# One core of Trainium2, attention into a mixture of experts: the first token list from two groups instead of three, and the order of the first weight loads

## The chip, the cores and the metric

The kernel runs on one core of one Trainium2 chip. The core has five engines with an instruction queue each, which run side by side and wait for one another by semaphores: PE (TensorE, matrix products; its weight loads are shown apart as PEld), DVE (VectorE), ACT (ScalarE), POOL (GpSimd) and SP (SyncE, which here only issues DMA transfers). The metric is the device time of one execution in microseconds, with its input and output in device memory; lower is better. The time before is 1149.84 us, the median of three runs (1148.15 to 1151.22).

## The reference

Attention over 8 batches and 8 heads with queries that are averaged in pairs, and behind it a mixture of experts in which each token goes to the one expert with the largest logit:

```python
q_pool = q.reshape(B, H, S // 2, 2, D).mean(axis=3)      # B = H = 8, S = 1152, D = 64
scores = matmul(q_pool, k^T) / sqrt(D)
attn   = exp(scores - max(scores)); attn /= sum(attn) + 1e-9
x      = matmul(attn, v)  ->  reshaped to (4608, 512)     # 8 batches x 576 queries, 8 heads x 64
logits = x @ w_gate + modality_bias[modality_id]          # 8 experts
e      = argmax(logits); gate = softmax(logits)[e]
out    = gate * (relu(x @ w1[e]) @ w2[e])                 # w1: 8 x 512 x 1024, w2: 8 x 1024 x 512
```

Everything is float32 at the interface.

## The kernel before, in words

**Attention.** The work is cut into 32 pairs: a pair is one head of two neighbouring batches. A pair has 18 steps, and Python loops over the 576 steps and writes the instructions of PE, ACT, DVE and POOL in exactly that order (the order of these four engines is set by hand; SP's order is left to the planner of the framework, which places each transfer by when it expects its operands to be ready). In a pair PE makes 24 score tiles (L879, L880), ACT takes the exponential of each (L881, result Pe), and PE multiplies with the values in three products per tile (L938 to L940), the third with the low bits of the exponentials, Pl. Pl is made on ACT for the first two thirds (L862) and on DVE for the rest (L864); in the last pairs the tables LOWS_LAST and P_LIST choose otherwise. The maxima of a pair (L812 on PE, L813 and L821 on DVE) are found one pair ahead; `row` turns them into one row and sends it to the right operand of the scores by a DMA on SP (L793). POOL splits queries and keys into high and low halves (L639, L646, L674) and scales the values (L761).

**Routing.** Eight pairs make one group of 1152 tokens (two batches, all heads); there are four groups, 0 to 3. `on_two` (L1449 and on) stores finished heads to a scratch tensor xs, and when a group's last head is stored, it appends the generator `route(g)` to the list `side`: it adds the logits up, finds each token's expert and its position within the expert. Behind group 2 it appends `first_list`, behind group 3 `other_list`. `first_list` counts how many full blocks of 256 tokens each expert has so far (`first_blocks`, L371 and on), places the tokens (`place`, L444 and on), and turns the places into lists of token numbers with small matrix products (`listing`, L519 and on; its operands in `operands`, L492 and on; `indices`, L542 and on). The result, the lists giA and siA of the first NA = 6 blocks, is what the first gathers of the expert stage need. `other_list` makes the lists of all other blocks from all four groups, later, beside the first six blocks.

**The side loop.** At the end of each step the attention loop advances the first generator of `side` once (L1143 to L1148). The number that it yields is how many steps pass before the next advance. So `route` (with rs = RS[g]) and the list are spread over the steps, a few small DVE or POOL instructions at a time, and each generator of the queue begins when the one ahead of it has ended. A negative yield, T_LIST, means "not before that step counted from the end of attention".

**The passage to the experts.** One step ahead of the last pair `early` takes over the buffers of raw queries, keys and values. `gather_first` first drains whatever is left in `side`, then POOL gathers the first block's tokens with giA (L1173). The first NF = 4 weight tiles of the first block are loaded by SP into the freed buffers (`load_first`, L1479 to L1483, which reads the block's expert from ownerA); ACT and DVE split them in the last pair (L1487, L1489).

**Experts.** 18 blocks of 256 tokens and one of 128 follow, each with eight weight tiles of 512 KB, gathered tokens, two matrix products in three parts each, and a scatter.

Of the kernel before, what the change touches and what calls it, by code (L numbers as in the profile page):

```python
# [9 lines left out]
F32 = mybir.dt.float32  # L10
# [12 lines left out]
P = 128  # L23
# [16 lines left out]
NR = 4  # L40
W3 = 3 * SQ
BANK = W3 // 4
T_LIST = -127
PL = 2
RS = (4, 4, 2, 2)
SLOW_P = 1
SLOW = 3
LAG = 3
# [2 lines left out]

LOWS = (((0, 1152, 'A', 2), (1152, 1728, 'D', 3)), ((0, 1152, 'A', 2), (1152, 1728, 'D', 3)))
LOWS_LAST = (((0, 864, 'D', 1), (864, 1728, 'D', 3)),)
P_LIST = {26: 0, 27: 0}
LOWS_LIST = [tuple(((0, 1152, 'A', 2), (1152, 1728, e, 3)) for e in x) for x in ('DDA', 'DA', 'A')]
D0 = 5
T_RT = 24
# [35 lines left out]
T = BATCH * SQ  # L93
DM = H * D
E = 8
F = 1024
XW = DM + 2
NT = 9
# [19 lines left out]
T_W0 = (1, 3, 2, 3)  # L118
# [7 lines left out]
NA = 6  # L126
# [35 lines left out]
class Router:  # L162
# [112 lines left out]
    def route(self, g, eng):  # L275

        nc, sm, rs = self.nc, self.sm, RS[g]
        while self.added[g] < H // 2:
# [165 lines left out]
    def place(self, nt, late):  # L444

        nc, sm = self.nc, self.sm
        be = lambda a: a.unsqueeze(1).broadcast_to([P, nt, E])
        yield
        wide = lambda i: sm.tile([P, nt, E], F32, name=f"ohp{nt}_{i}") if late else sm.tile([P, 3, NT, E], F32, name=f"wide{i}").rearrange("p q t e -> p (q t) e")
        oh = wide(0)  # L450
        nc.vector.tensor_tensor(oh, self.exp[:, 0:nt].unsqueeze(2).broadcast_to([P, nt, E]), be(self.ie), op=ALU.is_equal)
        yield
        w = wide(1)
        new = lambda name: sm.tile([P, NTT], F32, name=name)[:, 0:nt]

        def pick(o, of):

            nc.vector.scalar_tensor_tensor(w, oh, float(TB), be(of), op0=ALU.mult, op1=ALU.mult)
            yield
            nc.vector.tensor_reduce(o, w, op=ALU.add, axis=AX.X)  # L460
            yield

        lim, row, ok = new("lim"), new("row"), new("ok")
        yield from pick(lim, self.na)
        yield from pick(row, self.full if late else self.cumA[:, 0:E])
        nc.vector.tensor_tensor(row, row, self.pos[:, 0:nt], op=ALU.add)
        if late:
            yield from pick(ok, self.done)
            nc.vector.tensor_tensor(ok, self.pos[:, 0:nt], ok, op=ALU.is_ge)
            more = new("more")  # L470
            yield from pick(more, self.half)
            nc.vector.tensor_tensor(more, more, ok, op=ALU.mult)
            nc.vector.tensor_tensor(row, row, more, op=ALU.add)
        nc.vector.tensor_tensor(ok, self.pos[:, 0:nt], lim, op=ALU.is_ge if late else ALU.is_lt)
        yield
        nc.vector.scalar_tensor_tensor(row, row, float(2 * T), ok, op0=ALU.add, op1=ALU.mult)
        yield
        ri = sm.tile([P, NTT], I32, name="ri")[:, 0:nt]
        nc.vector.tensor_copy(ri, row)
        yield  # L480
        lo, hi = (sm.tile([P, NTT], I32, name=f"{x}i")[:, 0:nt] for x in ("lo", "hi"))
        nc.vector.tensor_single_scalar(lo, ri, P - 1, op=ALU.bitwise_and)
        nc.vector.tensor_single_scalar(hi, ri, 7, op=ALU.logical_shift_right)
        yield
        self.lo = sm.tile([P, NTT], BF16, name="lof")[:, 0:nt]
        nc.vector.tensor_copy(self.lo, lo)
        self.hi = sm.tile([P, NTT], F32, name="hif")[:, 0:nt]
        nc.vector.tensor_copy(self.hi, hi)
        yield
        nc.vector.tensor_single_scalar(self.hi, self.hi, -float(2 * T // P), op=ALU.add)  # L490
# [65 lines left out]
    def first_list(self):  # L556

        for _ in self.first_blocks():
            yield 1
        for _ in self.place(3 * NT, False):  # L560
            yield PL
        yield T_LIST
        acc = self.con.tile([P, 2, 2 * NA], F32, name="accA")
        yield from self.listing(3, 2 * NA, acc)
        self.idxA = self.indices(2 * NA, acc, "A")

    def other_list(self):
# [7 lines left out]
def attention(tc, ctx, att, ident, npairs, xpool, on_two, on_split, on_scale, jobs, side, set_pm, started, ahead, hip):  # L575
# [3 lines left out]
    nc = tc.nc  # L579
# [4 lines left out]
    sm = ctx.enter_context(tc.tile_pool(name="asm", bufs=3))  # L584
# [190 lines left out]
    def row(p, mp, u0, u1):  # L775

        n = u1 - u0
        m9 = sm.tile([P, 9], F32, name="m9")
        nc.vector.tensor_reduce(m9[:, 0:n], mp[:, u0:u1], op=ALU.max, axis=AX.X, negate=True)

        def finish():
            pt = some(0) if p else small()
            nc.tensor.transpose(pt[0:n, 0:P], m9[:, 0:n], ident)
            if now[0] > NSTEP:
                later_end(FD, lambda: put(pt))
            else:
                put(pt)

        def put(pt):
            mr = sm.tile([9, P], F16, name="mr", bufs=1)  # L790
            made.add((p, f"row{u1}"))
            nc.vector.tensor_scalar(mr[0:n], pt[0:n, 0:P], 1.0 / ROW, 16.0 * math.log(PSC) / ROW, op0=ALU.mult, op1=ALU.add)
            done = (nc.sync if p or u0 else nc.scalar).dma_start(out=B2[p % 2][D:D + 1, 2 * S + u0 * P:2 * S + u1 * P], in_=mr[0:n])  # L793
            if turns:
                with tc.issue_after(done.ins):
                    while turns:
                        turns.pop(0)()
        return finish
# [43 lines left out]
    def scores(p, j, r):  # L842
# [9 lines left out]
        s["P", j, r] = (word(F16, 1), Pl, i % NR)  # L852
        lows = LOWS_LAST if p == npairs - 1 else LOWS_LIST[P_LIST[p]] if p in P_LIST else LOWS if p else LOWS0
        lows = lows[i % len(lows)]
# [114 lines left out]
                on_two(p // 2, x2)  # L969
            later(XD, lambda: split_x(p, x2))  # L970

    turns = []
    now, flushed = [0], [-1]
    free = [0] * NR
    todo, at_end = {}, {}
# [8 lines left out]
    def at(t, p, fn, end=True):  # L984
        if 0 <= p < npairs:
            (at_end if end else todo).setdefault(max(t, 0), []).append(fn)
# [120 lines left out]
    if ahead:  # L1107
        last = (npairs - 1) * NSTEP
        room = []

        def early():
            a, *r = [pa.tile([P, S], F32, name="raw" + x) for x in "qqkkv"]
            room.extend(r)
            ahead[0](a)

        at(last + T_G0, 0, early)
        at(last + T_X0, 0, lambda: running.append(ahead[1](lambda: ps_max.tile([P, 512], F32, name="pm"))))
        for i in range(NF):
            at(last + T_W0[i], 0, lambda i=i: ahead[2](i, room[i]))
            at(last + T_W1[i], 0, lambda i=i: later_end(W1D, ahead[3](i)))  # L1120
    running, wait = [], 0
    for t in range(NSTEP * npairs):
        p, c18 = divmod(t, NSTEP)
        now[0] = t
        if jobs and c18 in JOBS:
            running.append(jobs.pop(0))
        for a in ORD[t % len(ORD)]:
            if a == "J":
                running[:] = [g for g in running if next(g, DONE) is not DONE]
            elif a == "F":  # L1130
                flush(t)
            elif a == "M":
                advance(mxq, 1)
            elif a == "X":
                advance(mxq, 3 if t < T_F else 1 if t < X_ALL or t % (X_IN if t < X_SOME else 4) == 0 or len(mxq) > 1 else 0)
            elif a == "N":
                scq.append(scores(p, *divmod(c18 // 3, 3)))
            elif a == "s":
                advance(scq, 1)
            elif a == "v":  # L1140
                advance(pvq, 2 if len(pvq) > 2 else 1)
        ends(t)
        if side and t >= wait:  # L1143
            r = next(side[0], DONE)
            if r is DONE:
                side.pop(0)
            else:
                wait = t + (r or 1) if (r or 1) > 0 else NSTEP * npairs + r  # L1148
# [14 lines left out]
def parts(j):  # L1163

    return range(2 if j < NBF else 1)


def gather_x(nc, rt, j, tile_):

    x = []  # L1170
    for h in parts(j):
        x.append(tile_(h))
        nc.gpsimd.indirect_dma_start(out=x[h][:, :], out_offset=None, in_=rt.xs[0:3 * NT * P if j < NA else T, :],  # L1173
                                     in_offset=bass.IndirectOffsetOnAxis(ap=index(rt, j, h)[0], axis=0))
    return x

# [260 lines left out]
def attention_moe(tc, att, ids, w_gate, bias, w1, w2, out):  # L1437
    nc = tc.nc
    with ExitStack() as ctx:
# [3 lines left out]
        rt = Router(tc, ctx, ident)  # L1443
# [3 lines left out]
        jobs, side, first = [], [], {}  # L1447

        def on_two(n, x2):  # L1449
            g, cc = divmod(n, H // 2)  # L1450
            eng = nc.gpsimd if n == NPAIR // 2 - 1 else nc.sync
            rt.store(g, cc, x2, eng)
            if cc == H // 2 - 1:
                side.append(rt.route(g, eng))
                if g == 2:
                    side.append(rt.first_list())
                if g == 3:
                    side.append(rt.other_list())
# [32 lines left out]
        ahead = (gather_first, turn_first, load_first, split_first) if NPAIR == BATCH // 2 * H else None  # L1491
# [54 lines left out]
```

## Time and profile before

| what | before |
|---|---|
| median of three runs | 1149.84 us (1148.15 to 1151.22) |
| the profiled execution, its own time | 1147.58 us |
| its span on the chip | 1145.8 us |
| granted TensorE clock, mean | 0.995 |
| attention, first to last exponential | 18.6 to 737.3 us |
| busy share PE, DVE, ACT, POOL | 97%, 85%, 80%, 37% |

A window of the profile is a stretch of the span, in microseconds from its start; for each engine it shows the busy time and, in brackets, how many instructions began in it. The pairs of attention can be told apart in it: each has 24 exponentials on ACT (L881), so pair p begins with exponential 24 p, and within a pair each three steps hold four of them. A "step" of the trace below is meant in that sense. An entry of a group of instructions gives line, engine, operation, output and inputs, shapes, count, busy time and mean duration in ns, and idle time ahead of it with what ended it. The durations on DVE overlap a little at their ends, so that they add to somewhat more than the busy time.

### The profile page before, as it was taken

The numbers are of one execution on the slowest core, as the hardware profiler recorded it, in microseconds if no ns is written. First come the engines' busy times: TensorE is split into PE (matmuls) and PEld (weight loads), VectorE is DVE, ScalarE is ACT, GpSimd is POOL, SyncE is SP. The second block draws the span as 40 slices with busy tenths as digits, with TensorE's granted clock in tenths as the row PEclk, the third lists the DMA queues.
The fourth block names the chain that finished last, engine by engine and source line by source line (L and its number), as shares of the span: only waits on it lengthen the run. The fifth ranks groups of instructions, "written<-read, shape, count | busy, mean of one in ns | idle before, by whom it ended". The sixth has DMA issues, their size and how long they took to land. (4 is left out here: it accounts for less than half of the span.)

```text
span 1145.8 us, 36648 instructions
## 1 busy us (share of the span) xinstructions
PE 1109.3 (97%) x15001; PEld 816.3 (71%) x15001; DVE 978.9 (85%) x1962; ACT 915.3 (80%) x1463; POOL 419.5 (37%) x408
## 2 busy tenths in 40 slices
PE   7999999999999999999999989999999999999995
PEld 3777777777777777777777767866676666766763
DVE  7999999999999999999999999888977667576661
ACT  5999999999999999999999989765656565565561
POOL 7753534444343454434445331232213221211201
PEclk9999999999999999999999999999999999999998
DMA  7776867857858759669668453699989999989970
GB/s 230 204 178 166 190 178 166 196 158 165 194 148 201 190 149 206 152 164 207 165 167 186 129 129 85 226 269 273 287 259 294 291 289 275 280 267 289 263 233 22
DMA packets 175568, 232.65 MB, mean 203 GB/s; under 512 B 92351, under 2 KB 126799, under 8 KB 175392
## 3 DMA queue, kind: packets, MB, share of 16 engines
q1 hardware_dynamic: 169254, 210.45, 70.3%
q0 software_dynamic: 6128, 19.78, 6.4%
q8 instruction: 119, 1.95, 0.7%
q14 instruction: 57, 0.47, 0.2%
q10 hardware_dynamic: 10, 0.00, 0.0%
HBM read 146.11 MB, written 19.18 MB: 144 GB/s over the span
## 5 line engine op out<-in xcount | busy, mean ns | idle before, releaser
L881 ACT ACTIVATE Pe<-psc 128x432 int32<-128x432 f32 x768 | 377.9, 526 | 43.1 <-PE psc L880 34.2
L813 DVE TENSOR_REDUCE mp<-pm 128x1 f32<-128x512 f32 x566 | 372.6, 684 | 14.4 <-PE pm L812 7.2
L938 PE MATMUL xp<-VH,Pe 128*128 128x65 f16 x2880 | 372.6, 193 | 0.0
L940 PE MATMUL xp<-VS,Pl 128*128 128x65 f16 x2880 | 371.9, 193 | 0.4 <-DVE Pl L864 0.4
L939 PE MATMUL xp<-vl,Pe 128*128 128x64 f16 x2880 | 370.7, 192 | 0.0
L939 PEld LDWEIGHTS <-Pe 128*128 128x128 f16 x2880 | 267.6, 98 | 87.6
L879 PE MATMUL psc<-B 128*128 128x432 f16 (+2 forms) x1152 | 304.0, 286 | 1.7 <-ACT Pe L881 1.5
L880 PE MATMUL psc<-B 65*128 65x432 f16 (+2 forms) x1152 | 304.7, 287 | 0.5 <-DMA B<-mr 0.5
L938 PEld LDWEIGHTS <-Pe 128*128 128x128 f16 x2880 | 271.9, 98 | 45.2 <-issue 7.0
L940 PEld LDWEIGHTS <-Pl 128*128 128x128 f16 x2880 | 266.5, 97 | 0.6 <-DVE Pl L864 0.5
L862 ACT ACTIVATE Pl<-Pe 128x1152 f16<-128x1152 uint16 (+1 forms) x190 | 219.3, 1154 | 6.0
L812 PE MATMUL pm<-hi,QB 128*128 128x512 f16 x566 | 213.7, 379 | 8.4 <-DVE mp L813 8.1
L674 POOL TENSOR_TENSOR lo<-rawk,hi 128x576 f16<-128x576 f32 (+1 forms) x68 | 88.0, 1298 | 196.0 <-ACT hi L658 185.6
L761 POOL TENSOR_SCALAR VH<-rawv,sc 128x512 f16<-128x512 f32 (+1 forms) x60 | 103.5, 1735 | 153.0 <-PE xp L940 73.7
L1287 PE MATMUL ph<-xpart,w1l 128*128 128x256 f16 x544 | 148.3, 273 | 0.0
L1285 PE MATMUL ph<-xpart,w1h 128*128 128x256 f16 x544 | 148.3, 273 | 0.0
L1286 PE MATMUL ph<-xpart,w1h 128*128 128x256 f16 x544 | 148.3, 273 | 0.0
L880 PEld LDWEIGHTS <-B 65*128 65x128 f16 x1152 | 112.9, 98 | 25.2 <-issue 2.5
L879 PEld LDWEIGHTS <-B 128*128 128x128 f16 x1152 | 112.5, 98 | 9.2 <-issue 3.8
L1291 DVE SCALAR_TENSOR_TENSOR hl<-ph,hh 128x512 f16<-128x512 f32 x72 | 49.7, 690 | 77.0 <-ACT hh L1290 76.3
L1290 ACT ACTIVATE hh<-ph 128x512 f16<-128x512 f32 x72 | 43.0, 598 | 87.2 <-PE ph L1287 87.2
L1333 PE MATMUL po<-w2h,hl 128*128 128x512 f16 x296 | 112.2, 379 | 0.0
(263 smaller groups left out, 1921.2 us busy)
## 6 DMA issues: line engine op xcount, KB each, us to landing
w2r<-in_w_dram SPq DMA_DIRECT2D x76, 512.0 KB
w1r<-in_w_dram SPq DMA_DIRECT2D x72, 512.0 KB
rawv<-in_att_dram SPq DMA_DIRECT2D x32, 576.0 KB
B<-hi SPq DMA_DIRECT2D x128, 144.0 KB
rawq<-in_att_dram SPq DMA_DIRECT2D x31, 576.0 KB
rawk<-in_att_dram SPq DMA_DIRECT2D x31, 576.0 KB
B<-qh SPq DMA_DIRECT2D x128, 72.0 KB
B<-lo SPq DMA_DIRECT2D x64, 144.0 KB
```

The costliest lines, as they stand in the source:

```text
L812: nc.tensor.matmul(pm, QB[p % 2][:, u], s["hi"][:, t * 512:(t + 1) * 512], start=True, stop=True)
L813: nc.vector.tensor_reduce(mp[:, u, t:t + 1], pm, op=ALU.max, axis=AX.X)
L862: nc.scalar.activation(low, rest, AF.Copy, scale=LOW)
L879: nc.tensor.matmul(o, b1[:, ks], b1[:, qs], start=True, stop=False, skip_group_check=True)
L880: nc.tensor.matmul(o, b2[:, ks], b2[:, qs], start=False, stop=True, skip_group_check=True)
L881: nc.scalar.activation(Pe[:, D + x0:D + x1], pt, AF.Exp, scale=1.0 / 16)
L938: nc.tensor.matmul(out, Ph[:, qs], vh[:, c, j, 0:D + 1], start=c == 0 and g == 0, stop=False, skip_group_check=True)
L939: nc.tensor.matmul(out[:, 0:D], Ph[:, qs], vl[:, c, j], start=False, stop=False, skip_group_check=True)
L940: nc.tensor.matmul(out, Pl[:, qs], vs[:, c, j, 0:D + 1], start=False, stop=c == NKC - 1, skip_group_check=True)
L1285: nc.tensor.matmul(o, hi[:, c, fs], xh[:, :, c], start=c == 0, stop=False)
L1286: nc.tensor.matmul(o, hi[:, c, fs], xl[:, :, c], start=False, stop=False)
L1287: nc.tensor.matmul(o, lo[:, c, fs], xh[:, :, c], start=False, stop=c == 3)
```

## The change

The first list is made from two groups (GA = 2), so it is queued behind `route(1)` and not behind `route(2)`; the arrays of `place` and `listing` cover 18 tiles of 128 tokens instead of 27, and the gathers of the first six blocks read only the first two groups' part of xs. All parts of the list now wait two steps between advances (PL); T_LIST is gone. `side` isn't advanced at the steps 5, 6, 7, 15 and 16 of any pair (FULL), which holds for the four `route` generators too as far as they run in attention. `route(2)` waits 4 steps instead of 2 (RS). P_LIST is empty, so pairs 26 and 27 make Pl as the others do. And the loads of the first block's first weight tiles are put behind the last pair's row of maxima in SP's queue (`issue_after` orders instructions within one engine's queue and adds no semaphore).

Counted through by these yields: `route(1)` runs from step 10 of pair 17 to step 17 of pair 19, `first_list` from step 0 of pair 20 to step 8 of pair 25, and `route(2)` from step 10 of pair 25 to step 17 of pair 27; nothing is in `side` in pairs 28 to 30. Before, `route(2)` runs from pair 25 to step 13 of pair 26, and `first_list` from there to the end of pair 30, where `gather_first` drains its rest.

```diff
-T_LIST = -127
 PL = 2
-RS = (4, 4, 2, 2)
+RS = (4, 4, 4, 2)
+GA = 2
+FULL = (5, 6, 7, 15, 16)
...
-P_LIST = {26: 0, 27: 0}
+P_LIST = {}
...
-        wide = lambda i: ... sm.tile([P, 3, NT, E], F32, name=f"wide{i}").rearrange("p q t e -> p (q t) e")
+        wide = lambda i: ... sm.tile([P, 3, NT, E], F32, name=f"wide{i}").rearrange("p q t e -> p (q t) e")[:, 0:nt]
...
         for _ in self.first_blocks():
-            yield 1
-        for _ in self.place(3 * NT, False):
             yield PL
-        yield T_LIST
+        for _ in self.place(GA * NT, False):
+            yield PL
         acc = self.con.tile([P, 2, 2 * NA], F32, name="accA")
-        yield from self.listing(3, 2 * NA, acc)
+        yield from self.listing(GA, 2 * NA, acc)
...
             done = (nc.sync if p or u0 else nc.scalar).dma_start(out=B2[...], in_=mr[0:n])
+            rows[p] = done.ins
...
+        def behind(ins, fn):
+            with tc.issue_after(ins):
+                fn()
...
-            at(last + T_W0[i], 0, lambda i=i: ahead[2](i, room[i]))
+            at(last + T_W0[i], 0, lambda i=i: behind(rows[npairs - 1], lambda: ahead[2](i, room[i])))
...
-        if side and t >= wait:
+        if side and t >= wait and c18 not in FULL:
             r = next(side[0], DONE)
...
-        ... in_=rt.xs[0:3 * NT * P if j < NA else T, :],
+        ... in_=rt.xs[0:GA * NT * P if j < NA else T, :],
...
-                if g == 2:
+                if g == GA - 1:
                     side.append(rt.first_list())
```

More of the change, by code (lines that the diff above doesn't have):

```diff
@@ L448, in place @@
         yield
-        wide = lambda i: sm.tile([P, nt, E], F32, name=f"ohp{nt}_{i}") if late else sm.tile([P, 3, NT, E], F32, name=f"wide{i}").rearrange("p q t e -> p (q t) e")
+        wide = lambda i: sm.tile([P, nt, E], F32, name=f"ohp{nt}_{i}") if late else sm.tile([P, 3, NT, E], F32, name=f"wide{i}").rearrange("p q t e -> p (q t) e")[:, 0:nt]
         oh = wide(0)
@@ L970, in evac @@
             later(XD, lambda: split_x(p, x2))
-    turns = []
+    turns, rows = [], {}
     now, flushed = [0], [-1]
@@ L1172, in gather_x @@
         x.append(tile_(h))
-        nc.gpsimd.indirect_dma_start(out=x[h][:, :], out_offset=None, in_=rt.xs[0:3 * NT * P if j < NA else T, :],
+        nc.gpsimd.indirect_dma_start(out=x[h][:, :], out_offset=None, in_=rt.xs[0:GA * NT * P if j < NA else T, :],
                                      in_offset=bass.IndirectOffsetOnAxis(ap=index(rt, j, h)[0], axis=0))
```

## The prediction, made before the changed kernel had run

> **What bounds the kernel now.** The page's first part says that PE, DVE and ACT are all nearly full, over the span:
>
> ```profile
> PE 1109.3 (97%) x15001; PEld 816.3 (71%) x15001; DVE 978.9 (85%) x1962; ACT 915.3 (80%) x1463; POOL 419.5 (37%) x408
> ```
>
> The change acts on attention alone, so I read windows with one pair of attention each next. Behind the length stand the busy times of PE, PEld, DVE, ACT and POOL. The pairs are 18 to 21 and 25 to 30:
>
> ```profile
> 422.33:445.34 23.01, 21.86 (x375) 16.76 (x372) 22.46 (x55) 21.53 (x40) 9.96 (x11) 1.00 0.86 187
> 445.34:467.88 22.54, 22.54 (x405) 17.55 (x402) 21.84 (x52) 21.02 (x38) 10.34 (x9) 1.00 0.61 155
> 467.88:489.50 21.62, 21.62 (x376) 16.78 (x373) 21.02 (x46) 20.81 (x38) 9.58 (x7) 1.00 0.85 190
> 489.50:511.65 22.15, 22.15 (x392) 17.20 (x390) 20.98 (x48) 20.91 (x38) 9.26 (x7) 1.00 0.60 166
> ...
> 577.05:599.36 22.31, 22.31 (x392) 17.32 (x391) 21.49 (x52) 21.07 (x39) 11.25 (x13) 1.00 0.59 166
> 599.36:623.66 24.30, 22.78 (x395) 17.62 (x394) 22.80 (x60) 22.25 (x39) 10.79 (x11) 1.00 0.82 186
> 623.66:647.81 24.15, 22.74 (x385) 17.25 (x382) 23.49 (x58) 22.26 (x39) 9.98 (x7) 1.00 0.50 137
> 647.81:671.22 23.41, 21.75 (x369) 16.61 (x367) 23.10 (x55) 21.49 (x38) 9.45 (x7) 1.00 0.67 138
> 671.22:696.88 25.66, 23.13 (x395) 17.57 (x392) 25.38 (x57) 21.61 (x38) 8.26 (x6) 1.00 0.34 84
> 696.88:717.67 20.79, 20.28 (x383) 16.23 (x380) 19.72 (x51) 19.03 (x35) 3.43 (x2) 1.00 0.53 122
> ```
>
> Pairs 20 and 21 have nothing of the side loop: 21.62 us for an even and 22.15 us for an odd pair, with DVE idle for 0.60 and 1.17 us, ACT for 0.81 and 1.24 us. So no engine has much room, and an extra instruction on DVE is paid in time. Pairs 18 and 19 hold one `route`: 1.39 + 0.39 = **1.78 us**. Pairs 25 to 29 hold `route(2)` and most of the list: 0.16 + 2.68 + 2.00 + 1.79 + 3.51 = **10.14 us** above the clean pairs. Pair 30 has fewer maxima, so it has no clean twin; the rest of the list lies in it, on 1.07 us of idle DVE time, and I put it at 0.4 us (bounds 0 and 0.8).
>
> **Part 1: P_LIST goes.** It gave ACT two of DVE's low parts in each of pairs 26 and 27. The low parts on ACT alone (L862), pairs 20 and 26:
>
> ```profile
> 467.88:489.50 21.62, 6.99 (x6) 1.00 0.85 190
> ...
> 599.36:623.66 24.30, 8.35 (x8) 1.00 0.82 186
> ```
>
> 1.36 us of ACT are more than the 0.81 us that it had free, and what DVE saved for it is 0.49 us a part:
>
> ```profile
> L864 DVE TENSOR_SCALAR Pl<-Pe 128x576 f16<-128x576 uint16 x27 | 13.2, 488 | 0.5 <-ACT Pe L881 0.5
> ```
>  Without P_LIST and without the list, pairs 26 and 27 should read as 18 and 19 do; that is in the sum as their return to 1.78 us.
>
> **Part 2: where the list is dear.** Three stretches of a pair, by its exponentials (steps 0 to 6, 7 to 9, 10 to 17); clean pair 20, the middle of clean pair 21, then the later two of pair 18 (`route`), all of 28 (list) and the middle of 29:
>
> ```profile
> 467.88:475.63 7.75, 7.75 (x134) 5.99 (x131) 7.39 (x19) 7.07 (x14) 5.33 (x4) 1.00 0.59 136
> 475.63:479.80 4.17, 4.17 (x80) 3.33 (x79) 4.14 (x8) 4.13 (x8) 1.59 (x1) 1.00 0.64 170
> 479.80:489.50 9.70, 9.70 (x169) 7.45 (x166) 9.50 (x21) 9.61 (x18) 2.65 (x2) 1.00 1.14 241
> ...
> 497.36:501.76 4.40, 4.40 (x91) 3.57 (x90) 4.37 (x10) 4.21 (x8) 1.28 (x1) 1.00 0.79 244
> ...
> 430.08:434.72 4.64, 3.83 (x64) 2.90 (x63) 4.61 (x8) 4.20 (x8) 1.98 (x2) 1.00 0.80 220
> 434.72:445.34 10.62, 10.28 (x178) 7.87 (x178) 10.37 (x28) 10.11 (x19) 2.65 (x5) 1.00 1.10 210
> 647.81:655.39 7.58, 7.55 (x128) 5.75 (x126) 7.40 (x21) 6.96 (x15) 5.23 (x4) 1.00 0.55 129
> 655.39:660.20 4.81, 3.93 (x64) 2.97 (x63) 4.78 (x11) 4.21 (x8) 1.38 (x2) 1.00 0.71 180
> 660.20:671.22 11.02, 10.28 (x178) 7.88 (x178) 10.92 (x25) 10.32 (x18) 2.85 (x2) 1.00 0.73 126
> ...
> 679.36:686.08 6.72, 4.29 (x82) 3.38 (x82) 6.69 (x11) 4.41 (x7) 1.52 (x2) 1.00 0.41 118
> ```
>
> The middle is where a pair loses time at once: 0.47 us in 18, 0.64 in 28, 2.32 in 29. What ran just ahead of it was planned for step 4 or 5 (L301 and L303 in pair 18, L482 and L483 in 28, one L502 in 29). That L502 on DVE and its neighbours, and POOL at the same time:
>
> ```profile
> 678.38 1.42 DVE L502 TENSOR_TENSOR ol<-lof,lane 128x384 bf16<-128x384 bf16 x1
> ...
> 682.00 1.54 DVE L771 TENSOR_SCALAR VS<-VH 128x1152 f16<-128x1152 f16 x1
> ```
>
> ```profile
> 678.11 1.28 POOL L674 TENSOR_TENSOR lo<-rawq,qh 128x576 f16<-128x576 f32 x1
> 681.73 1.50 POOL L674 TENSOR_TENSOR lo<-rawk,hi 128x576 f16<-128x576 f32 x1 [2.34 <-ACT hi L658]
> ```
>
> L502 began behind the first L674 and ended only after it, at 1.42 us instead of 0.54; being late, DVE then met the second L674 with L771. The page "SBUF — State Buffer" of the Trainium skill, under "Who interferes with whom", has this as a rule: a DVE instruction with two SBUF inputs and a GpSimd instruction that reads SBUF exclude each other, and the later one stands until the other has ended; the trace agrees here, with 1.42 us. By that rule a planned step 8 is no better than a step 5, which is the last rival below. Other instructions, in pair 28 and over the whole list:
>
> ```profile
> L508 DVE TENSOR_TENSOR o<-hif,col 128x108 f32<-128x108 f32 x1 | 1.1, 1060 | 0.0
> ...
> L476 DVE SCALAR_TENSOR_TENSOR row<-row,ok 128x27 f32<-128x27 f32 x1 | 0.6, 587 | 0.0
> L502 DVE TENSOR_TENSOR ol<-lof,lane 128x384 bf16<-128x384 bf16 x1 | 0.5, 539 | 0.0
> ```
>
> ```profile
> L451 DVE TENSOR_TENSOR wide<-exp,ie 128x216 f32<-128x216 f32 x1 | 1.5, 1464 | 0.0
> L458 DVE SCALAR_TENSOR_TENSOR wide<-wide,cutA 128x216 f32<-128x216 f32 x1 | 1.4, 1428 | 0.0
> L514 DVE TENSOR_SCALAR r<-o,part 128x108 bf16<-128x108 f32 x3 | 0.8, 265 | 0.0
> ...
> L458 DVE SCALAR_TENSOR_TENSOR wide<-wide,na 128x216 f32<-128x216 f32 x1 | 0.4, 367 | 0.0
> ...
> L490 DVE TENSOR_SCALAR hif<-hif 128x27 f32<-128x27 f32 x1 | 0.2, 166 | 0.0
> ```
>
> L458 runs 367 ns alone and 1428 ns beside POOL, so a collision adds some 1.0 us (L502: 0.88). **The list after**: 21 small instructions and 2 copies of sums at about 0.17 us, 5 indices at 0.17, five wide ones of `place` at 18/27 of the width (estimate 0.30 between 367 ns and a small one), 6 of L502 at 0.54, 2 of L508 and 4 of L513/L514 at 0.26: 4.8 + 1.5 + 3.2 + 1.6 = **11.1 us**. By the counted steps, about 2.6 us of it are planned for steps 0 to 4, where pair 28 shows no loss (7.58 against 7.75, with L476's 0.59 us inside); I price them at 0.15. The other 8.5 us fall on 8 to 14 and 17. Collisions: POOL starts an L674 near step 8 and an L674 and L639 near 13, and the list has a two-input instruction at step 8 in pairs 20, 21, 23, 24, 25 and at step 14 in 21, 22, 23; at 0.6 to 1.0 us I take 6.5 us for the eight (none: 0; all full: 8). That makes 15.0 us outside the cheap steps.
>
> The price per us: pair 28's last stretch lost 1.32 us for 2.3 us (L490, L502 twice, L508), 0.57. Pair 25 lost 0.16 us for 0.51 us more of busy DVE, 0.31, and odd pairs have twice the idle time. I take **0.45**, so 6.8 + 0.4 = **7.2 us** in pairs 20 to 25; the bounds are 0.25 (4.2) and 0.65 (10.2).
>
> **Part 3: `route`.** Its L301 moves from step 5 to 8 and its other parts by up to 6 steps. The 0.47 us of the middle go, but the same instructions are paid behind it, perhaps with a collision; the small ones of step 16 move to step 1, where they are free. I take -0.2 us for each of three (bounds -0.7 and +0.3). RS = 4 for group 2 changes only when it ends; nothing waits for it before the last pair.
>
> **Part 4: the loads and the gather.** SP's queue and POOL's at the last pair:
>
> ```profile
> 713.02 0.79 SPq L793 DMA_DIRECT2D B<-mr  x1
> 713.86 1.31 SPq L922 DMA_TRANSPOSE xt<-x  x1
> 715.40 0.40 SPq L1483 DMA_DIRECT2D rawq<-in_w_dram  x1
> ```
>
> ```profile
> 718.27 1.44 POOL L1173 DMA_INDIRECT rawq<-xs,giA  x1 [15.60 <-DVE siA L553]
> ```
>
> The loads already stand behind the row, so the edge removes nothing: 0 us. It is needed only because ownerA is ready five pairs sooner. Behind them on SP stand only transfers of the experts' stage, and the splits of the last pair, which wait for the loads, keep their distance to the row. The gather no longer waits for siA; nothing reads it earlier, so 0 us. The blocks stay 18 and one half: on the reference's inputs, two groups hold eight full blocks, and six are used.
>
> **The sum**: -10.14 - 0.4 + 1.78 + 7.2 - 0.6 = **-2.2 us**, or 1143.6 us of span and 1145.4 us for an execution like the profiled one (1147.58). The median before stands 2.26 us above that execution; to it the same is added: **1147.6 us**. With the bounds: -10.9 + 1.8 + 4.2 - 2.1 = -7.0 and -10.1 + 1.8 + 10.2 + 0.9 = +2.8, so 1142.8 to 1152.6.
>
> **The rivals.**
> *The list nearly vanishes in the idle time.* Pairs 20 to 25 have 5.3 us of idle DVE time (3 x 0.60 + 3 x 1.17). For it: pair 25's 0.31. Against it: pair 18 left as much idle time (23.01 - 22.46 = 0.55) as pair 20. At the lower bounds: -6.5 us, 1143.3.
> *It is DVE's amount of work that counts, not its place.* Over pairs 25 to 29 DVE is busy 11.28 us more than in clean ones, for 10.14 us: 0.9. The list loses a third of `listing` (3 x 0.54 + 5 x 0.26 = 2.9 us) and P_LIST's end gives DVE four low parts back, about 2.0 us: -0.9 x 0.9 = -0.8, 1149.0. Against it: the free steps 0 to 4.
> *FULL packs the list onto POOL* (slower). What waited for steps 5 to 7 all comes at step 8, on the L674 that starts there, and each such hit drags the next DVE work into POOL's next instruction, as in pair 29: 2.32 us. With all five of them: 11.6, plus 0.45 x 8.5 for the rest and 0.4: 15.8; -10.5 + 1.8 + 15.8 = +7.1, 1156.9. Each such hit costs 1.7 us more than the forecast gives it (2.32 less 0.45 x 1.4), so the second uses up the forecast's 2.2 us and from the third on the kernel is slower. Against it: pair 27's L451 collided in the same place, and that pair lost 2.00 us in all, P_LIST included.
> *The edge doesn't do what it says*: that is my forecast for it.
>
> **How the numbers follow.** Forecast 0.42, vanishing 0.26, amount 0.17, packed 0.15. A measurement of this kernel tells 0.3%, 3.45 us, from no change. Faster: the vanishing case and a third of the forecast's range, 0.40. Slower: the packed case and a little of the others, 0.17. Same: 0.43. The likeliest case's own range is 1142.8 to 1152.6; the range is 1142.0 to 1153.5, which leaves out the packed case's far end and little else.
>
> **What would show it.** Pairs 28 and 29 at 21.62 and 22.15 us; pairs 26 and 27 near 23.0 and 22.5 with six L862 each; pairs 20 to 25 longer by 7 us together, most where DVE's list instructions take over 1 us beside L674 or L639; L793 ahead of L1483. It is wrong if pairs 20 to 25 grow by more than 10 or less than 4 us, if pairs 28 and 29 keep a loss, or if SP's order shifts elsewhere and L880 waits for the row.

## The result: slower by 0.8%

| | before | after |
|---|---|---|
| median, six runs each (three of before are new) | 1149.16 us (1148.15 to 1151.22) | 1158.17 us (1156.65 to 1160.49) |
| profiled execution, its span | 1147.58, 1145.8 us | 1156.65, 1154.9 us |
| ratio, with its 95% interval | | 1.0081 (1.0068 to 1.0094) |

The forecast was 1147.6 us in 1142.0 to 1153.5: wrong in size and in sign. In the changed kernel the lines of attention stand one further down (the exponential is L882, the reduction of maxima L814), those of the passage to the experts five (the first loads are L1488). The busy times of the page have hardly moved; PE's share fell by a point:

```profile
PE 1113.0 (96%) x14992; PEld 817.7 (71%) x14992; DVE 983.9 (85%) x1959; ACT 913.6 (79%) x1459; POOL 419.3 (36%) x408
```

Windows of the changed kernel, one pair in each, columns as in the prediction; the pairs are 10, 11, 20, 21, 28, 29 and 31 (26 and 27 are as 10 and 11):

```profile
245.40:267.67 22.27, 21.55 (x375) 16.68 (x372) 21.87 (x51) 21.18 (x40) 8.59 (x8) 1.00 0.89 175
267.67:292.52 24.85, 22.95 (x405) 17.77 (x402) 23.74 (x55) 21.08 (x38) 11.46 (x12) 1.00 0.58 157
...
470.81:493.96 23.15, 21.87 (x375) 16.77 (x372) 22.84 (x54) 21.36 (x38) 9.27 (x7) 1.00 0.81 170
493.96:517.94 23.98, 22.83 (x395) 17.48 (x392) 23.70 (x55) 21.38 (x37) 9.80 (x7) 1.00 0.56 160
...
660.62:682.24 21.62, 21.62 (x376) 16.78 (x373) 21.01 (x45) 20.80 (x38) 9.56 (x7) 1.00 0.81 152
682.24:704.40 22.16, 22.16 (x392) 17.20 (x390) 20.99 (x48) 20.89 (x38) 7.89 (x6) 1.00 0.40 97
...
724.29:746.38 22.09, 19.18 (x355) 15.95 (x352) 15.74 (x32) 16.33 (x33) 2.67 (x2) 0.92 0.47 158
```

Pairs 28 and 29 are clean, as said. Pairs 20 to 25 pay for the list, pair 11 (as 19 and 27) is longer than before though it has no list at all, and in the last pair the granted clock falls to 0.92. Behind the last exponential come 408.5 us, as before: the experts' stage doesn't take part. So the whole result lies in the lengths of pairs. Here they are, for the runs that tell most (one run starts pair 10 up to 3 us earlier or later than another, so lengths of pairs are better compared than spans):

| pairs, us | before | after | a2: `route` free of FULL | a4: a2, list off nine steps | best5: a4, read early |
|---|---|---|---|---|---|
| 10 + 11 | 45.55 | 47.12 | 45.55 | 45.54 | 45.55 |
| 18 + 19 | 45.55 | 46.98 | 45.54 | 45.54 | 45.54 |
| 20 to 25 | 131.48 | 142.69 | 141.98 | 132.86 | 132.57 |
| 26 + 27 | 48.45 | 47.12 | 45.53 | 44.46 | 44.44 |
| 28 + 29 | 49.07 | 43.78 | 43.78 | 46.97 | 46.98 |
| 30 | 20.79 | 19.89 | 19.89 | 19.90 | 19.90 |
| 31 | 19.59 | 22.09 | 20.54 | 20.35 | 18.91 |

After less before is 9.2 us over these rows, 9.1 in the span. Three things make it.

**The list.** DVE's groups in pairs 20 to 25 of the changed kernel (mean ns of one behind the comma):

```profile
L759 DVE SCALAR_TENSOR_TENSOR vl<-rawv,sc,VH 128x640 f16<-128x640 f32 x6 | 7.4, 1234 | 0.0
...
L452 DVE TENSOR_TENSOR wide<-exp,ie 128x144 f32<-128x144 f32 x1 | 1.4, 1385 | 0.0
...
L487 DVE CAST lof<-loi 128x18 bf16<-128x18 int32 x1 | 1.2, 1180 | 0.0
L390 DVE TENSOR_SCALAR left<-cumA 128x8 f32<-128x8 f32 x1 | 1.1, 1147 | 0.0
```

L390 has eight elements a partition, its neighbours of that size take 160 ns, and it took 1147. L759 isn't of the list but stands now too: in pairs 20 to 24 of before these took 874 ns, so the six lose some 2.2 us. One such hit, L452 in pair 21, on DVE, POOL and PE:

```profile
504.44 1.83 POOL L674 TENSOR_TENSOR lo<-rawk,hi 128x576 f16<-128x576 f32 x1 [2.51 <-ACT hi L658]
...
505.05 1.39 DVE L452 TENSOR_TENSOR wide<-exp,ie 128x144 f32<-128x144 f32 x1
...
506.36 0.68 DVE L814 TENSOR_REDUCE mp<-pm 128x1 f32<-128x512 f32 x1
...
507.09 0.38 PE L813 MATMUL pm<-hi,QB 128*128 128x512 f16 x1 [1.11 <-DVE mp L814]
```

L452 stands until POOL's L674 has ended; the reduction L814 queued behind it starts a microsecond late, and PE, which needs the buffer that L814 empties, waits 1.11 us. Over pairs 20 to 25 PE's waits for DVE's maxima come to (total us, how many, the longest)

```profile
PE pm L813 <- DVE mp L814: 5.8, 6, 1.2
PE pm L783 <- DVE m L779: 1.4, 2, 1.2
```

that is one of 1.0 to 1.2 us in every pair (in pair 24 it is the one for L779, the last step of the maxima), and a shorter one or two. Before, PE has no such wait in pairs 20 to 24. These waits are 7.2 us of the 11.4 us by which pairs 20 to 25 exceed clean ones. In the rest PE counts as busy (134.9 us instead of 131.3); the list's own 18 small products are 0.8 us of it, and what makes the remainder is not broken down.

**`route` behind FULL.** Pair 11 of the changed kernel, the middle, on POOL, DVE and PE:

```profile
270.25 0.19 POOL L323 COPY gt<-ts 128x9 f32<-128x9 f32 x1 [2.15 <-DVE ts L320]
...
275.95 1.29 POOL L674 TENSOR_TENSOR lo<-rawq,qh 128x576 f16<-128x576 f32 x1
278.02 1.28 POOL L674 TENSOR_TENSOR lo<-rawk,hi 128x576 f16<-128x576 f32 x1 [0.78 <-ACT hi L658]
...
276.48 1.08 DVE L865 TENSOR_SCALAR Pl<-Pe 128x576 f16<-128x576 uint16 x1
...
278.45 1.53 DVE L759 SCALAR_TENSOR_TENSOR vl<-rawv,sc,VH 128x640 f16<-128x640 f32 x1
...
276.88 0.38 PE L331 MATMUL pm<-oh,on 128*128 128x72 bf16 x9
277.21 0.60 PE L267 MATMUL pm<-wgs,xt 128*128 128x24 bf16 x18
278.58 0.38 PE L813 MATMUL pm<-hi,QB 128*128 128x512 f16 x1 [0.77 <-DVE mp L814]
280.63 0.38 PE L821 MATMUL pm<-hi,QB 128*128 128x128 f16 x4 [1.12 <-DVE mp L814]
```

Kept off steps 5 to 7, `route`'s ten products (the nine of L331 and one of L329) now come at step 8, 9.2 us into the pair instead of 2.0, beside the 18 products of the logits (L267), and both take a buffer from the pool of the maxima. POOL runs behind as well, since its copy L323 stood in line for DVE's L320, and its late L674 meets DVE's L865 (1.08 us) and L759 (1.53 us). The even pairs 10 and 26 gain 0.8 us from FULL (22.27 for 23.03), the odd ones lose three times that; 18 and 19 together lose 1.4 us.

**The last pair.** SP's queue and what waits for it:

```profile
719.46 0.79 SPq L793 DMA_DIRECT2D B<-mr  x1
720.30 1.32 SPq L923 DMA_TRANSPOSE xt<-x  x1
723.29 0.38 SPq L1488 DMA_DIRECT2D rawq<-in_w_dram  x1
```

```profile
L1486 SPq TENSOR_LOAD <-ownerA x1: 1108/1108/1108, 721.7 to 721.7; - x1
```

```profile
730.84 1.06 ACT L1492 ACTIVATE w1h<-rawk 128x1024 f16<-128x1024 f32 x1 [2.44 <-DMA rawk<-in_w_dram]
...
732.36 0.28 PE L880 MATMUL psc<-B 128*128 128x288 f16 x1 [2.07 <-ACT Pe L882]
```

The row (L793) is ahead of the loads (L1488), as before. But the edge catches everything that `load_first` issues, also the reading of the block's expert into a register: 1.11 us of SP between transpose and loads. It was at 631.1 us before. ACT waits 2.44 us for the loads (0.94 before), PE 2.07 us for ACT. Two windows of 3.41 us, the one with that wait and the next:

```profile
729.62:733.03 3.41, 1.34 (x28) 1.14 (x26) 1.10 (x1) 2.19 (x5) 0.00 (x0) 1.00 0.33 131
733.03:736.44 3.41, 3.41 (x55) 2.57 (x52) 2.95 (x8) 2.02 (x4) 0.00 (x0) 0.50 0.02 5
```

The granted clock (third number from the end) is at 0.50 behind PE's wait, for 3.4 us. The last section works out when that happens; it decides several of the comparisons below.

### The profile page after: what moved, and what is told of

It reads as the page before. It is cut to its first block, busy times and chain, and to the rows that moved or that the text cites. A ratio compares the mean times of both kernels' runs of the same rounds, so it can differ in the third digit from the quotient of the medians.

```text
span 1154.9 us, 36627 instructions
## 1 busy us (share of the span) xinstructions
PE 1113.0 (96%) x14992; PEld 817.7 (71%) x14992; DVE 983.9 (85%) x1959; ACT 913.6 (79%) x1459; POOL 419.3 (36%) x408
## 5 line engine op out<-in xcount | busy, mean ns | idle before, releaser
L882 ACT ACTIVATE Pe<-psc 128x432 int32<-128x432 f32 x768 | 379.4, 526 | 51.4 <-PE psc L881 42.1
L814 DVE TENSOR_REDUCE mp<-pm 128x1 f32<-128x512 f32 x566 | 372.6, 684 | 12.7 <-PE pm L813 6.4
L880 PE MATMUL psc<-B 128*128 128x432 f16 (+2 forms) x1152 | 304.8, 287 | 3.2 <-ACT Pe L882 3.0
L939 PEld LDWEIGHTS <-Pe 128*128 128x128 f16 x2880 | 272.4, 98 | 49.0 <-issue 10.7
L813 PE MATMUL pm<-hi,QB 128*128 128x512 f16 x566 | 214.0, 379 | 9.1 <-DVE mp L814 8.6
L863 ACT ACTIVATE Pl<-Pe 128x1152 f16<-128x1152 uint16 x186 | 216.5, 1164 | 5.9
L674 POOL TENSOR_TENSOR lo<-rawk,hi 128x576 f16<-128x576 f32 (+1 forms) x68 | 89.7, 1322 | 200.0 <-ACT hi L658 190.7
L761 POOL TENSOR_SCALAR VH<-rawv,sc 128x512 f16<-128x512 f32 (+1 forms) x60 | 103.2, 1729 | 150.5 <-PE xp L941 87.3
L880 PEld LDWEIGHTS <-B 128*128 128x128 f16 x1152 | 112.6, 98 | 7.8 <-issue 2.3
L1337 PE MATMUL po<-w2l,hh 128*128 128x512 f16 x296 | 112.4, 380 | 0.0
```

What stands on the lines that cost most here:

```text
L813: nc.tensor.matmul(pm, QB[p % 2][:, u], s["hi"][:, t * 512:(t + 1) * 512], start=True, stop=True)
L814: nc.vector.tensor_reduce(mp[:, u, t:t + 1], pm, op=ALU.max, axis=AX.X)
L863: nc.scalar.activation(low, rest, AF.Copy, scale=LOW)
L880: nc.tensor.matmul(o, b1[:, ks], b1[:, qs], start=True, stop=False, skip_group_check=True)
L882: nc.scalar.activation(Pe[:, D + x0:D + x1], pt, AF.Exp, scale=1.0 / 16)
L939: nc.tensor.matmul(out, Ph[:, qs], vh[:, c, j, 0:D + 1], start=c == 0 and g == 0, stop=False, skip_group_check=True)
```

## The experiments

All diffs stand against the changed kernel, except c1's. Where nothing else is said, a time is one execution beside one of before on the same chip (1148.00 for a1 to a4, 1147.53 for b1 to b4).

### What FULL does to `route`: a2, a3, b3, d1

a2 keeps FULL for the list alone:

```diff
-        if side and t >= wait and c18 not in FULL:
+        if side and t >= wait and not (c18 in FULL and side[0].__name__ == "first_list"):
```

> The changed kernel, but the five steps are left out for first_list only; route runs at every step as before. Theory B (the steps left out push route's matrix products from step 2 to step 8, where the logits' products of the same pair run, and the maxima then lack buffers and DVE time): pairs 11, 19 and 27 return from about 24.4 to 24.9 us to 22.5, pairs 10, 18 and 26 are at 23.0; the span falls by about 4.5 us to 1150.4. Rival (the loss in pairs 11, 19 and 27 comes from something else that the change does, such as the waits of 4 steps or the order of the generators): they stay near 24.5, span 1154.9.

Measured: 1148.75 us, span 1147.0. Pair 11, and the instructions that had collided, in a2:

```profile
267.62:290.15 22.53, 22.53 (x405) 17.55 (x402) 21.82 (x52) 21.00 (x37) 10.31 (x9) 1.00 0.59 153
```

```profile
276.21 0.46 DVE L865 TENSOR_SCALAR Pl<-Pe 128x576 f16<-128x576 uint16 x1
...
277.55 0.88 DVE L759 SCALAR_TENSOR_TENSOR vl<-rawv,sc,VH 128x640 f16<-128x640 f32 x1
```

The three routes are back at 45.55 us for two pairs, and 4.6 us of the loss are gone. That FULL is what hurts `route` is shown. Of the other 3.3 us of a2's gain 1.55 lie in the last pair, whose clock didn't fall although the edge and the late register read are still there: chance, as the last section shows.

a3 leaves FULL and gives `route`'s products another PSUM pool, so that they take no buffer from the maxima:

```diff
-        pr = self.pm(4)[:, 0:(NT + 1) * E].rearrange("p (t e) -> p t e", e=E)
+        pr = self.pm(9)[:, 0:(NT + 1) * E].rearrange("p (t e) -> p t e", e=E)
```

> The changed kernel with one difference: route's matrix product (L328, L330) goes to a PSUM buffer of the value products' pool and not to one of the three that the maxima use. All instructions and their order stay. Theory B1 (at step 8 two of the three buffers of the maxima are held, by route's product and by the logits, so PE waits for DVE to free the third): the 2.5 us that pairs 11, 19 and 27 lose in steps 8 and 9 fall below 1 us each, span down by 4 to 6 us to about 1150. Rival B2 (DVE is simply late there, with the collision of L759 and three more instructions): the loss stays at 2.5 us, span 1154.9.

Measured: 1153.04 us. Pairs 11, 19 and 27 at 23.8 us each, against 24.85, 24.42 and 24.85 (with the even pair beside it, each is 0.9 to 1.0 us shorter). So the shared buffers are some 1.0 us of each odd pair's loss of 2.3; PE's wait of 1.12 us at L821 is gone, the one at L813 stays (0.7).

b3 tries the other suspect: POOL's copy L323 goes to DVE, so that POOL doesn't stand in line.

```diff
-        nc.gpsimd.tensor_copy(gt[:, :, 1], ts2[:, 1:2].broadcast_to([P, NT]))
+        nc.vector.tensor_copy(gt[:, :, 1], ts2[:, 1:2].broadcast_to([P, NT]))
```

> The changed kernel with one instruction moved: route's copy of the inverse scale (POOL L323 in the changed kernel), which waits for a DVE reciprocal that the left-out steps delay, is made on DVE. Theory E (POOL stands at that copy, with L639, L761, L646 and L674 of the next pair queued behind it; they come 2 us later and then meet DVE's L865 and L759): L639 starts about 2.5 us sooner relative to the pair, L865 and L759 in steps 7 to 9 of pairs 11, 19 and 27 are back at 0.46 and 0.87 us, and these pairs fall from 24.4 to 24.9 to 23.8 or below (what is left is the PSUM buffer); span down by 3 to 5 us. Rival F (only DVE's own lateness and PSUM matter there): the pairs stay above 24.3, span 1154.9.

Measured: 1161.85 us, slower still: pairs 11 and 19 at 27.2 us, 27 at 25.7. In pairs 11 and 19 the granted clock is at 0.50 for 3.4 us, in 27 it isn't, which is their difference of 1.5 us; so the copy on DVE itself costs 0.8 us a pair (25.66 against 24.85). POOL is on time (its first L674 of the stretch at 274.42) and that L865 takes 0.46 us again, but an L865 at the pair's start now stands beside L639 (1.27 us), and the next collision is worse:

```profile
278.16 1.92 DVE L759 SCALAR_TENSOR_TENSOR vl<-rawv,sc,VH 128x640 f16<-128x640 f32 x1
```

d1 has both edits:

> The changed kernel with route's matrix product in the value products' PSUM pool and route's copy on DVE instead of POOL, together. Each alone gave 1153.0 (pairs 11, 19, 27 at 23.8) and 1161.9 (27.2, 27.2, 25.7). If PSUM and the late POOL instructions each hold part of the loss and the second run was worse only because its longer stalls met the scarce PSUM buffers: pairs 11, 19 and 27 at 22.5 to 23.2, span about 1150. If the copy's place on DVE is bad in itself: 24 or more, span above 1154.

Measured: 1158.13 us, pairs 11, 19 and 27 at 24.66 each, with the clock at 1.00; worse than a3 alone. The two edits simply add up: 1.0 us less for the buffers, 0.8 more for the copy. The theory that the held POOL queue makes the rest of the loss has fallen: taking that wait away changes which instruction of DVE meets L674, not that one does. What remains beside the PSUM buffers, 1.3 us of each odd pair in a3 (23.82 less 22.53), lies by the traces in such meetings; which one decides isn't settled. A warning goes with it. In a run without the edge (c2 below) pair 19 took 26.36 us instead of 24.42 (24.87 in a1), and in a1 pair 11 took 26.37 instead of 24.85. These are no other meetings: in a1's pair 11 L865 and L759 take 1.08 and 1.52 us and PE waits 0.78 and 1.13 us, as in the changed kernel. The granted clock is the difference:

```profile
277.62:281.03 3.41, 1.69 (x23) 1.24 (x23) 2.94 (x4) 0.92 (x2) 1.28 (x1) 1.00 0.91 286
281.03:284.44 3.41, 3.41 (x38) 2.46 (x35) 2.60 (x7) 2.80 (x4) 0.00 (x0) 0.50 0.24 89
```

and at the same place of the changed kernel:

```profile
275.65:279.06 3.41, 2.64 (x66) 2.17 (x65) 3.38 (x6) 2.69 (x4) 2.54 (x3) 1.00 0.53 72
279.06:282.47 3.41, 2.29 (x34) 1.83 (x33) 2.94 (x7) 1.57 (x3) 0.24 (x1) 1.00 0.88 345
282.47:285.88 3.41, 3.41 (x64) 2.71 (x63) 3.13 (x9) 3.38 (x7) 0.00 (x0) 1.00 0.02 5
```

So a pair with PE waits of this size can be 1.3 to 1.5 us longer or not, in one kernel, and a single run doesn't tell such a difference from an effect of the edit.

### What the list costs, and where: a4, b1, b2

All three have a2's edit, and more steps in FULL: a4 the nine of this diff, b1 of the new ones only step 8, b2 only 12 to 14.

```diff
-FULL = (5, 6, 7, 15, 16)
+FULL = (5, 6, 7, 8, 12, 13, 14, 15, 16)
```

> As the run in which only first_list leaves steps out, but it leaves out 8, 12, 13 and 14 as well, so that it advances only at steps 0 to 4, 9 to 11 and 17. Theory C (the list is dear because its instructions with two SBUF inputs stand still beside POOL's L674 and L639, near steps 8 and 13): nearly no list instruction takes over 0.7 us, and the pairs with the list (about 20 to 27) lose 5 to 6 us together instead of 11.3; span about 1145. Rival D (DVE is full, and what the list costs is its amount of work wherever it stands): the list's instructions run at their own length, but the pairs lose 10 us or more together; span 1150 or above.

> As the run in which only first_list leaves steps out (1148.75 us), with step 8 left out too, but not 12 to 14. The run that leaves out 8 and 12 to 14 came to 1143.23. If POOL's L674 on the keys near step 8 does most of the harm: about 1145, and the list's DVE time falls from 17.5 us to about 15. If it is the pair of L674 and L639 near step 13: about 1148.

> The other half: 12 to 14 left out too, but not 8. If the harm sits near step 13: about 1145; if near step 8: about 1148. If each half alone brings nearly all of the 5.5 us, then it is not the stalls but the smaller number of steps per pair that helps (the list spread over more pairs).

| | after | a2 | b1 | b2 | a4 |
|---|---|---|---|---|---|
| time, us | 1156.65 | 1148.75 | 1152.38 | 1148.34 | 1143.23 |
| DVE time of the list's 45 instructions, us | 18.8 | 17.5 | 17.7 | 16.5 | 12.85 |
| the list's last instruction (L554) in pair | 25 | 25 | 26 | 27 | 27 |
| from pair 20 to that pair, above clean ones, us | 11.4 | 10.7 | 9.8 | 8.9 | 2.2 |

(In after and b1 some 1.5 us of the time are the clock's fall in the last pair.) In a4 pairs 20 to 25 take 132.86 us, 1.6 above clean ones, and PE's waits for L814 there are gone. The groups of the list in pairs 20 to 27 of a4's successor best5, which has the same steps:

```profile
L452 DVE TENSOR_TENSOR wide<-exp,ie 128x144 f32<-128x144 f32 x1 | 0.3, 302 | 0.0
...
L487 DVE CAST lof<-loi 128x18 bf16<-128x18 int32 x1 | 0.2, 171 | 0.0
L390 DVE TENSOR_SCALAR left<-cumA 128x8 f32<-128x8 f32 x1 | 0.2, 163 | 0.0
```

The same instructions, the same operands, 1147 against 163 ns: the difference is POOL. And the time lost follows the list's DVE time steeply. Down to a4 it falls by 9.2 us for 5.95 us from the changed kernel, by 8.5 for 4.65 from a2, by 7.6 for 4.85 from b1 and by 6.7 for 3.65 from b2; in b1 and b2 the last pairs hold the beginning of `route(2)` too, which may be up to 2 us of theirs. So the list's standing costs **1.2 to 1.8 us of the kernel per us**, while the list that hardly stands costs 2.2 us for 12.85, or 0.17. A part of that price is the standing of others that the list pushes into POOL: L759 loses 2.2 us in the changed kernel, 2.4 in a2, 3.2 in b1, 0.4 in b2 and nothing in a4. With it counted, the price is 1.1 to 1.2 in the changed kernel and a2, and 0.7 to 1.6 over all four: about 1 us per us.

A rival was that not the place but the thinner spreading helps. b2 spreads the list into the same pair 27 as a4 and loses 8.9 us, of which at most 2 are `route(2)`'s: spreading is not what does it. Nor does one half of the steps: what step 8 refuses comes a few steps later, beside the other L674 and L639. Groups of b1's list, from pair 20 to the end of 27:

```profile
L459 DVE SCALAR_TENSOR_TENSOR wide<-wide,cutA 128x144 f32<-128x144 f32 x1 | 1.2, 1153 | 0.0
L487 DVE CAST lof<-loi 128x18 bf16<-128x18 int32 x1 | 1.1, 1085 | 0.0
...
L452 DVE TENSOR_TENSOR wide<-exp,ie 128x144 f32<-128x144 f32 x1 | 0.3, 296 | 0.0
...
L390 DVE TENSOR_SCALAR left<-cumA 128x8 f32<-128x8 f32 x1 | 0.2, 157 | 0.0
```

L452 and L390 are freed, L459 stands in their place, L487 stands as before. b1 is even slower than a2: pairs 20 to 25 take 2.9 us less, but 26 and 27, where `route(2)` begins elsewhere in its pair and PE once waits 1.4 us for the queries' DMA, take 49.0 us instead of 45.5, and the clock falls in the last pair (1.5 us).

a4 has a price of its own: `route(2)` now falls into pairs 28 and 29 and loses 3.2 us there instead of 1.78.

### The edge: a1, c2

a1 reads the expert into the register earlier, in `gather_first`, and leaves the loads behind the edge:

```diff
+            first["e"] = nc.sync.value_load(rt.ownA[0:1, 0:1], min_val=0, max_val=E - 1)
...
-                first["e"] = nc.sync.value_load(rt.ownA[0:1, 0:1], min_val=0, max_val=E - 1)
```

> The changed kernel, but SP reads the first block's expert from ownerA into its register when the gather is traced, outside the edge; only the four loads stay behind the last row. Theory A (the edge has pulled the register read, 1.4 us with its two register operations, into SP's queue between the row and the loads, and the last pair pays for it): the read stands tens of us earlier, the loads begin 1.4 us sooner after the row, ACT's wait for rawk falls from 2.44 to about 0.9 us, the last pair from 22.1 to about 19.6 us and the span from 1154.9 to 1152.4. Rival (the loads are slow for another reason, the earlier gather or other transfers): the last pair stays at 22 us, span 1154.9.

Measured: 1156.61 us, no gain in all, but the last pair is 19.19 us instead of 22.09, with its clock at 1.00; the planner now places the reading at 504.8 us, and ACT's wait shrinks:

```profile
731.42 1.06 ACT L1493 ACTIVATE w1h<-rawk 128x1024 f16<-128x1024 f32 x1 [0.39 <-DMA rawk<-in_w_dram]
```

Its 2.9 us were lost again in pairs 11 and 27, which came out 1.5 and 1.3 us longer because the clock fell to 0.50 in both, as told above. What the edit does in the last pair is 2.9 us, or 1.2 to 1.4 against a4 and a2 (20.35 and 20.54 us), whose clock stayed at 1.00 there.

c2 takes the edge away:

```diff
-            at(last + T_W0[i], 0, lambda i=i: behind(rows[npairs - 1], lambda: ahead[2](i, room[i])))
+            at(last + T_W0[i], 0, lambda i=i: ahead[2](i, room[i]))
```

> The changed kernel without the edge on the first weight loads (the first block's loads are free in SP's queue). If the edge is needed, the loads and their register read move ahead of the last row in SP's queue, wait there for the freed buffers, and the row comes late: the last pair or pair 30 gets longer than in the changed kernel, by some us. If the edge is only a cost: the register read runs early, the loads stand where they were, and the last pair falls from 22.1 to about 19.2 us (span 1152).

Measured: 1162.57 us, beside 1147.8 for before. SP's queue and PE's wait without the edge:

```profile
712.76 0.42 SPq L1488 DMA_DIRECT2D rawq<-in_w_dram  x1
...
720.10 4.36 SPq L923 DMA_TRANSPOSE xt<-x  x1
724.55 0.81 SPq L793 DMA_DIRECT2D B<-mr  x1
```

```profile
PE psc L881 <- DMA B<-mr: 3.3, 1, 3.3
```

The loads go out first, the transpose behind them takes 4.36 us instead of 2.06, the row comes behind it, 1.6 us later in the pair than in the changed kernel, and pair 30 with the wait for the row takes 23.27 instead of 19.89 us. (The later issue explains half of PE's 3.3 us; the rest lies between the row's issue and its use and isn't resolved.) The other 2.5 us by which c2 is slower are the clock, which fell in pairs 19 and 27, less 0.6 us in the last pair. So with a list that is ready early the edge is worth some 3.4 us; it is only its catch that costs: the register read, free of the edge, stands at 505.7 us here.

### P_LIST alone: c1

Against the kernel before:

```diff
-P_LIST = {26: 0, 27: 0}
+P_LIST = {}
```

> The kernel before with P_LIST emptied and nothing else: pairs 26 and 27 make all their low parts as the others do. The prediction took the table for a cost (1.36 us more on ACT in each of two pairs than ACT had free). If so, pairs 26 and 27 become shorter, by 1 to 2 us together, and the span falls from 1145.8 to about 1144.5. If DVE is what counts, as the list's price of 1.3 us for each us of stall in the later runs suggests, the 0.98 us per pair that go back to DVE make them longer by 1 to 3 us: 1147 to 1149.

Measured: 1148.31 us beside 1147.8 (1147.02 to 1149.14): no difference that can be told, and neither of the two expectations is borne out. Pairs 26 and 27 lose 0.5 us less, pairs 28 and 31 0.6 and 0.9 more.

### The two repairs together: b4_best, best5

a4 and a1 in one kernel; best5 is the same kernel in five rounds.

> The list off the nine steps, route at every step, and the register read ahead of the edge: the run at 1143.23 with the last pair mended. By theory A the last pair falls from 20.35 to about 19.2 us: 1142.0. If the register read costs nothing when the loads have slack: 1143.2.

> The list off nine steps, route at every step, register read ahead of the edge, timed against the kernel before: one look gave 1142.8 beside 1147.5. Theory C and A together: 0.4% faster than before, ratio 0.996, and 1.2% faster than the changed kernel.

Measured: b4 1142.82 us in one execution; best5 **1141.54 us** (1140.74 to 1142.30) beside 1147.80 (1147.02 to 1149.14) for before: ratio 0.9945 (0.9932 to 0.9959). It beats both kernels. Pairs 28, 29 and 31 of best5:

```profile
644.09:667.67 23.58, 22.17 (x375) 16.91 (x372) 23.15 (x52) 21.54 (x40) 10.17 (x9) 1.00 0.63 139
667.67:691.07 23.40, 23.16 (x405) 17.77 (x402) 22.68 (x56) 21.35 (x38) 9.79 (x10) 1.00 0.40 93
...
710.97:729.88 18.91, 17.77 (x355) 15.05 (x352) 15.70 (x32) 16.18 (x34) 2.68 (x2) 1.00 0.48 161
```

What is left is in the first two rows: 3.2 us above clean pairs for one `route`, which costs 1.78 in pairs 18 and 19.

## Why the prediction was wrong, step by step

- **What bounds the kernel, and the 10.14 us that the old list cost**: right. Pairs 28 and 29 came out at 21.62 and 22.16 us, pair 30 at 0.9 us less (0.4 said).
- **Part 1, P_LIST**: the return of pairs 26 and 27 to 1.78 us didn't come in the changed kernel (3.35), but not for P_LIST: with `route` free of FULL they are at 23.01 and 22.52, 1.76 above clean. That P_LIST cost anything, c1 doesn't show.
- **Part 2, the amount**: the list without standing was put at 11.1 us; in a4 it is 12.85, of which L379, L459, L503 and L509 stand for some 1.6, so 11.2. (These four meet POOL's L761, a TENSOR_SCALAR of 1.6 to 1.9 us, and are held for 0.4 us each, not until it ends; that happened beside L674 and L639.) The collisions were put at 6.5 us in eight places; they are 7.6 (18.8 less 11.2), in more and partly other places: the prediction counted two-input instructions, and L379, L381, L390 and L487, with one, stood for 2.7 us. The rule of the Trainium skill that was weighed there ("SBUF — State Buffer", "Who interferes with whom") names casts and scalar operations in their two-port modes beside the two-input ones; the trace agrees, with L390's 1147 and L487's 1180 ns; that these two ran in such a mode, no run here shows.
- **Part 2, the price**: this step failed. One price, 0.45 us per us, was put on all that lies outside the cheap steps, and collisions were counted as more DVE work. They aren't: work that is placed well cost 0.17 (2.2 us for 12.85), the list's standing 1.2 to 1.8, for a standing DVE holds the reduction that PE waits for, and pushes L759 into POOL's next instruction. Pairs 20 to 25 lost 11.4 us instead of 7.2, beyond the upper bound of 10.2. The prediction had the number before it: L502's 1.42 us in the old pair 29, in a stretch that lost 2.32 us.
- **Part 3, `route`**: this step failed most, -0.2 us each with +0.3 as the bound, measured +1.6, +1.4 and +1.6 (a2 takes all of it away). DVE's instructions were followed to their new steps; the ten products on PE, and the buffer that they take from the maxima beside the logits' own, were not looked at, nor what POOL's wait for L320 holds up.
- **Part 4, the edge**: "removes nothing: 0 us" was right for the order of the DMAs, and c2 shows that it is needed, as said. But `load_first` issues a register read besides its DMA, and the edge moved it from 631 to 722 us. Cost with what follows: 2.5 us in pair 31 (2.9 by a1). Of this 1.5 us are the fallen clock, which the prediction didn't have and which the same late read didn't bring in a2 and a4 (20.54 and 20.35 us). The gather and the 18 and a half blocks: no change, as said.
- **The sum**: of the 11.3 us between forecast (-2.2) and result (+9.1), 5.2 are `route`, 4.2 the list (0.5 of it by the 1.1 us of collisions more, the rest its price), 2.5 the last pair, and -0.5 pair 30.
- **The rivals**: "packed onto POOL" gave +7.1 us, nearest to the +9.1 of the spans; a hit costs PE near 1 us in every pair, as it said in kind. But it put all 15.8 us on the list, which cost 11.4; that the sums come near each other is owed to `route` and the register, which it didn't have. "Vanishing" (0.31 us per us) is what the list does once it is off POOL. "The amount of work" fell: best5 and the changed kernel make the same list with the same 45 instructions, at 1.9 us above clean (pairs 20 to 27) and 11.4 us (pairs 20 to 25).

## What to carry to other kernels

Split the cost of side work on a full engine into work and standing, and price them apart: here the one cost 0.2 us per us and the other about 1, so a plan of steps must be checked against the other engine's long instructions, all of them at once. A rule that keeps work off some steps hits everyone who uses the same loop, and on every engine that he issues to: list the buffers, too. And an ordering edge holds all that is issued under it; take register reads out of it. Look at the granted clock of each stretch before an edit is blamed or praised for 1.5 us.

## What the runs showed of the hardware that was not expected

**The granted clock halves when PE stands for about 1.5 us in one window of 3.41 us.** In each of the 14 traces all changes of the clock lie on one grid with a step of 3.41 us, whose place differs from trace to trace; both windows shown for the last pair, and the five for pair 11, are cells of it. In attention, from 100 us on, the clock was at 0.50 in the next cell in all 12 cases in which PE's idle time in a cell at full clock was 1.53 us or more, and never where it was 1.52 or less. (At the start, with 1.41, and in the experts' stage, with 1.54 to 1.70, it went otherwise several times, so the limit isn't sharp.) So a wait counts by how much of it falls into one cell, and several short waits add up: in a1's pair 11 the waits of 0.78 and 1.13 us leave 1.69 us busy in one cell, in the changed kernel they are divided over two.

PE's longest wait in the last pair (for ACT, ahead of the product that is L880 after; in c2 in pair 30, for the row), its idle time in the cell with most of it, and whether the clock fell to 0.50 behind it:

| | after | a3 | b1 | b3 | d1 | c2 | a2 | a4 | b2 | c1 |
|---|---|---|---|---|---|---|---|---|---|---|
| PE's wait, us | 2.07 | 2.59 | 2.03 | 1.91 | 2.62 | 3.29 | 1.91 | 1.72 | 2.03 | 1.51 |
| idle in the cell, us | 2.07 | 1.85 | 2.03 | 1.91 | 2.16 | 2.50 | 1.32 | 1.45 | 1.47 | 1.09 |
| to 0.50 | yes | yes | yes | yes | yes | yes | no | no | no | no |
| pair 31, us | 22.09 | 22.18 | 22.04 | 21.95 | 23.57 | 21.48 | 20.54 | 20.35 | 20.65 | 20.53 |

The same wait of 2.03 us did it in b1, where it lies in one cell, and not in b2, where it is divided. A fall makes about 1.5 us of a pair; that the changed kernel's six executions, from 1156.65 to 1160.49 us, differ by it is likely, but only one of them was profiled. The Trainium skill ("TensorE: Matmul & The Clock Gate", Part 1) puts the fall behind an idle window of about 3.4 us whose start isn't tied to the work. The window and its free start agree with these traces; that it must be idle as a whole does not: about 1.5 of 3.41 us was enough.

**A DMA transpose behind weight loads on the same queue** took 4.36 and 3.77 us in c2, against 2.06 and 1.32 us in the changed kernel, where they stand ahead of the loads. Other transposes of the last pairs took 1.3 to 3.2 us in before, the changed kernel, c2 and best5.
